# First two units as one 256-column MLP group, a clock model in the ordering loop, and a new table of places

## The chip, the cores and the metric

The kernel runs on one core of a Trainium2 chip. The core has a matrix engine (TensorE, PE in the profile; its weight loads are PEld), a vector engine (VectorE, DVE), a scalar engine (ScalarE, ACT), GpSimd (POOL), and SyncE (SP), whose queue issues nearly all transfers here. Each engine works through its own queue in the order in which the program wrote it. The metric is the device time of one execution in microseconds (us).

## What is computed

Three stages follow each other: a linear recurrence with complex decay (called attention in the code), an MLP with squared ReLU, and a gated MLP behind an RMS norm.

```python
# attention: q, k, v, a_re, a_im are [4, 8, 768, 48]
mag = sqrt(a_re**2 + a_im**2); scale = minimum(mag, 0.999) / (mag + 1e-6)
for t in range(768):
    S_re, S_im = ar*S_re - ai*S_im + k[t] (x) v[t], ar*S_im + ai*S_re
    y[t] = q[t] @ S_re
x = y as [3072, 384]
# MLP 1: w_in [384, 2048], w_out [2048, 384]
x = maximum(x @ w_in, 0)**2 @ w_out
# MLP 2: w_gate, w_val [384, 1536], w_out [1536, 384]
xn = x / sqrt(mean(x*x) + 1e-6) * rms_g
out = (silu(xn @ w_gate) * (xn @ w_val)) @ w_out
```

## The kernel before

**Units.** The sequence is cut into 24 units of 128 positions (4 batches x 6 chunks); unit u belongs to batch u % 4. Each unit goes through these steps. `chain` (L415) builds the decay products on DVE: `norm` with help of ACT, seven steps of `step` (XY, then two A rows, L363 to L370), `tot` (a PE transpose, L380), four levels `plevel` on DVE, `back` (PE, L429), six products, and `inv`. `prod` (L497) makes the tiles KP and QP; `dtr` (L527) transposes them on PE into dk and dq; `score` (L540) multiplies them on PE and masks the result on DVE (st, L542); `yy` or, for units 0 and 1, `yy_direct` (L575) makes the unit's output on PE (yps); `state` (L606) updates the running state. The output becomes the MLP's input xs, split in a high and a low part (L905 and L907 for units 0 and 1, L843 and L845 for the others).

**Chains and groups.** `SETS` says which units share a chain: unit 0 alone, unit 1 alone, then pairs. `GROUPS` says which units share the columns of a matmul of MLP 1: `[0]`, `[1]`, `[2, 3]`, `[4, 5]`, `[6, 7]`, and then four units at a time. So the matmuls of MLP 1 have 128, 128, 256, 256, 256 and from then on 512 columns.

**MLP 1.** For each group there are 16 steps f. `mlp_h` issues nine matmuls (three passes of high and low parts times three row tiles, L943), then ACT computes r (L950), gs (L953) and h (L955), and DVE the low part of gs (L957). `mlp_x` issues nine more (L963) from gs. Nine such matmuls are called a block below. A block of the first group needs the units' xs, and each f its weights: these arrive as 16-bit words and are put together by `convert` (ACT L638, DVE L640 into cr, ACT L870, and the low part on DVE, L882, or for even f on PE, L876 and L877).

**MLP 2.** Six groups of 512 columns, 12 steps f each, of one block g, one block v (L1135) and one block o (L963). us, the input of o, has three buffers.

**What sets the order.** The class `Plan` runs a small list scheduler when the program is written. Each job (a step of one unit, one block, one load) is a generator that yields `Op`s with an engine, a cost and what they need. `Plan.job` gives it a place: a due time from the loops, plus `PRI` of its kind, plus an amount from the table `SHIFT` for the n-th job of that kind. `Plan.run` takes the engine times by its own cost functions, picks among the jobs that could start soonest the one with the lowest place, and writes its instructions. Its order is the order of every engine's queue on the chip. Its costs include a rule on TensorE's clock: after a pause of more than 2.0, the next 3.0 of matmul cost count double (`self.cold`).

Of the kernel before, what the change touches and what calls it, by code (L numbers as in the profile page):

```python
# [1 line left out]

# [20 lines left out]
NU = B * NC  # L23
# [16 lines left out]
    load_a=-32, load_qk=-31, load_v=-28, chain=-32, decay=-32, prod_k=-24, prod_q=-24, join=-24, dtr_k=-24, dtr_q=-24,  # L40
    score=-24, y=-24, fix=-24, split=-24, turned=-24, state=-23.6, mlp_h=-60, mlp_x=-59.9, store_x=-60, load_w=-347,
    convert=-12, load_x=-72, rms=-72, mlp_g=-60, mlp_v=-59.9, mlp_o=-59.8, store=-60, load_w2=-16, convert2=-16,
)
SHIFT = dict(
    chain=((0, 6, 42.5), (6, 11, 30), (11, 12, 29), (12, 13, 28.5),),
    convert=((1, 2, -32.5), (3, 4, -18), (4, 6, -3), (6, 8, -45.5), (8, 16, -3),),
    convert2=((0, 18, -10.5),),
    decay=((0, 8, 60.5), (8, 9, -20.5), (9, 13, 60.5),),
    dtr_k=((2, 7, -38.5), (7, 11, -57.5), (11, 12, -111.5), (12, 21, -92.5), (21, 24, -54),),
    dtr_q=((0, 5, 2.5), (5, 6, -101.5), (6, 13, -34.5), (13, 14, -101.5), (14, 15, -104), (15, 19, -101.5),  # L50
        (19, 21, -104), (21, 23, -114.5), (23, 24, -10.5),),
    fix=((0, 9, 4.5), (9, 11, -1.5), (11, 22, 4.5),),
    join=((36, 38, 7), (48, 102, 48.5), (102, 114, 81),),
    load_a=((7, 11, -62),),
    load_w=((6, 8, -5), (11, 14, -24.5), (14, 15, -13.5), (15, 16, -78.5),),
    mlp_g=((5, 40, -4.5), (40, 47, -7.5),),
    mlp_h=((7, 10, 5), (10, 13, -13.5), (13, 16, 5), (31, 34, 11.5), (76, 78, 28.5),),
    mlp_o=((0, 15, 3), (15, 28, -37.5), (28, 65, 3), (65, 72, 2.5),),
    mlp_x=((55, 58, 46), (126, 128, -1),),
    prod_k=((0, 24, -39),),  # L60
    prod_q=((0, 1, 26), (1, 6, 66.5), (6, 23, 26), (23, 24, 24),),
    rms=((0, 6, 19.5),),
    score=((39, 48, -19),),
    split=((1, 8, 22.5), (8, 9, 49.5),),
    state=((0, 10, 10), (10, 12, 65.5), (12, 13, 40.5), (13, 20, 10),),
    store=((7, 16, -1.5),),
    store_x=((3, 6, 2.5), (16, 18, 50.5),),
    turned=((2, 3, 25.5), (6, 9, 4), (9, 10, -23.5), (10, 11, 17.5), (11, 19, -23.5), (19, 20, 4),),
    y=((13, 24, 22),),
)  # L70
LAND = 2.2
AFTER = {"pe": 0.2, "dve": 0.115, "act": 0.095, "pool": 0.12}
URGENT, NEAR = -250, 0.3
LATE = {"pe": 2.0}
SETS = [[0], [1]] + [[u, u + 1] for u in range(2, NU, 2)]
SET = {u: (s, us.index(u)) for s, us in enumerate(SETS) for u in us}
GROUPS = [[0], [1], [2, 3], [4, 5], [6, 7]] + [list(range(u, u + 4)) for u in range(8, NU, 4)]
OF = {u: (g, us.index(u)) for g, us in enumerate(GROUPS) for u in us}
DIRECT = (0, 1)


def mm(k, n):
    return k * (0.006 + 0.0004375 * n)
# [6 lines left out]
def act(n):  # L90
    return 0.097 + n / 1200


def after(of, to):
    return 0.0 if of == to == "pe" else AFTER.get(of, 0.0)


class Op:


    def __init__(self, eng, cost, need=(), acq=(), rel=(), done=None, mb=0.0, p=0.0, free=False):
        self.eng, self.cost, self.need, self.acq, self.rel = eng, cost, need, acq, rel
        self.done, self.mb, self.p, self.free = done, mb, p, free


class Plan:
# [6 lines left out]
    def __init__(self, counts):  # L113
        self.counts = counts
        self.taken = {r: 0 for r in counts}
        self.back = {r: [] for r in counts}
        self.t = {}
        self.free = {}
        self.bus = 0.0
        self.cold = 0.0  # L120
        self.jobs = []
        self.kinds = {}
        self.log = []

    def job(self, kind, at, gen, need=()):
        n = self.kinds[kind] = self.kinds.get(kind, -1) + 1
        at += PRI[kind] + sum(d for lo, hi, d in SHIFT.get(kind, ()) if lo <= n < hi)
        self.jobs.append([at, len(self.jobs), gen, None, 0.0, need])

    def ready(self, j):  # L130

        t, op = j[4], j[3]
        for n in (*j[5], *op.need):
            end, eng = self.t[n]
            t = max(t, end + after(eng, op.eng))
        for r in op.acq:
            k = self.taken[r] - self.counts[r]
            if k >= 0:
                if k >= len(self.back[r]):
                    return None  # L140
                end, eng = self.back[r][k]
                t = max(t, end + after(eng, op.eng))
        return t

    def run(self):
        live = list(self.jobs)
        while live:
            best = {}
            for j in live:
                if j[3] is None:  # L150
                    if not all(n in self.t for n in j[5]):
                        continue
                    j[3] = next(j[2])
                if not all(n in self.t for n in j[3].need):
                    continue
                r = self.ready(j)
                if r is not None:
                    s = max(r, self.free.get(j[3].eng, 0.0))
                    fresh = r + LATE.get(j[3].eng, 0.0) * (j[3].p == 0.0)
                    best.setdefault(j[3].eng, []).append((s, j[0] + j[3].p, j[1], j, fresh))  # L160
            pick = []
            for c in best.values():
                s0 = min(x[0] for x in c)
                now = [x for x in c if x[0] <= s0 + 0.02]
                now += [x for x in c if s0 + 0.02 < x[0] <= s0 + NEAR and x[1] <= URGENT]
                old = [x for x in now if x[4] <= max(s0, x[0])]
                pick.append(min(old, key=lambda x: x[1:3]) if old else min(now, key=lambda x: (x[4], *x[1:3])))
            s, _, _, j, _ = min(pick, key=lambda x: x[:3])
            op = j[3]
            self.log.append((s, op.eng, op.cost, j[2].__name__, j[0]))  # L170
            cost = op.cost
            if op.eng == "pe":
                if s - self.free.get("pe", 0.0) > 2.0:
                    self.cold = 3.0
                cost += min(cost, self.cold)
                self.cold = max(0.0, self.cold - op.cost)
            end = self.free[op.eng] = s + cost
            for r in op.acq:
                self.taken[r] += 1
            if op.mb:  # L180
                self.bus = max(self.bus, end) + op.mb * 4.0
                end = self.bus + LAND
            for r in op.rel:
                self.back[r].append((end, op.eng))
            if op.done is not None:
                self.t[op.done] = (end, op.eng)
            j[3] = next(j[2], None)
            j[5] = ()
            if j[3] is None:
                live.remove(j)  # L190
            elif j[3].free:
                j[4] = max(j[4], s)
            else:
                j[4] = end + after(op.eng, j[3].eng)
# [616 lines left out]
def kernel_body(ctx: ExitStack, tc, q, k, v, vt, a_re, a_im, w, rms_g, out):  # L811
# [80 lines left out]
    def xs_tile(u):  # L892
        g, i = OF[u]
        if i == 0:
            xs_t[g] = sb.tile([128, 2, KT, len(GROUPS[g]) * CH], F32R, tag="xs", name="xs", bufs=2)
        return xs_t[g]
# [38 lines left out]
    def mlp_h(g, f):  # L935
        n = len(GROUPS[g]) * CH
        yield Op("pe", mm(9, n), acq=["h"], rel=["xs"] if f == F1 - 1 else [], done=("h", g, f), p=MLP_PE)
# [30 lines left out]
    def mlp_x(g, f):  # L968
        n = len(GROUPS[g]) * CH
        yield Op("pe", mm(9, n), acq=[] if f else ["xg"], rel=["gs"], done=("x", g, f), p=MLP_PE)  # L970
        if f == 0:
            x_ps[g] = [psx.tile([128, n], F32, tag=f"x{e}", name=f"x{e}") for e in range(KT)]
        turned_out(x_ps[g], lambda bb: part(f, 1, bb), g_t.pop((g, f)), f == 0, f == F1 - 1)

    def store_x(g, e):
        n = len(GROUPS[g]) * CH
        yield Op("act", act(n), acq=["r"], done=("xc", g, e))
        x = sb.tile([128, n], F32, tag="r", name="x1", bufs=2)
        nc.scalar.copy(out=x, in_=x_ps[g][e])
        yield Op("sp", 0.65, rel=["r"], mb=0.27, done=("xnd", g, e))  # L980
        nc.sync.dma_start(xnd[e * 128:(e + 1) * 128, GROUPS[g][0] * CH:GROUPS[g][0] * CH + n], x)

# [283 lines left out]
```

## Time and profile before

| | us |
|---|---|
| median of 3 runs | 1145.66 |
| lowest, highest | 1144.36, 1145.94 |
| the profiled execution, its own time | 1144.84 |
| its span, first to last instruction | 1142.9 |
| PE busy in the span | 1096.0 (96%) |
| DVE busy | 705.8 (62%) |
| ACT busy | 570.9 (50%) |

The profile is of one execution. A row of a timeline gives the start, the length and the number of equal instructions in a run; since matmuls overlap, the step from one block's start to the next one's start is what a block costs, not its length. The granted clock (PEclk) is a share of TensorE's full 2.4 GHz; 0.50 is its other level, 1.2 GHz. A share of busy time is a mean over a stretch: which engine sets the pace has to be read stretch by stretch.

### The profile page before, as it was taken

The numbers are of one execution on the slowest core, as the hardware profiler recorded it, in microseconds if no ns is written. First come the engines' busy times: TensorE is split into PE (matmuls) and PEld (weight loads), VectorE is DVE, ScalarE is ACT, GpSimd is POOL, SyncE is SP. The second block draws the span as 40 slices with busy tenths as digits, with TensorE's granted clock in tenths as the row PEclk, the third lists the DMA queues.
The fourth block names the chain that finished last, engine by engine and source line by source line (L and its number), as shares of the span: only waits on it lengthen the run. The fifth ranks groups of instructions, "written<-read, shape, count | busy, mean of one in ns | idle before, by whom it ended". The sixth has DMA issues, their size and how long they took to land.

```text
span 1142.9 us, 17676 instructions
## 1 busy us (share of the span) xinstructions
PE 1096.0 (96%) x6850; PEld 931.1 (81%) x6850; DVE 705.8 (62%) x1461; ACT 570.9 (50%) x1142; POOL 4.0 (0%) x14
## 2 busy tenths in 40 slices
PE   2788999999999999999999999999999999999997
PEld 1687899999998888888888888888888888888886
DVE  7969878999999989896522786452252332522221
ACT  4757657768657557554644895242142331421221
POOL 1000000000000000000000000000000000000000
PEclk9778899999999999999999999999999999999999
DMA  9821414423524524301002762001010010000001
GB/s 315 268 72 31 129 45 109 113 76 103 137 63 105 140 57 132 88 26 54 29 2 70 255 207 80 28 1 56 1 56 1 1 56 1 1 28 1 28 1 31
DMA packets 87452, 85.54 MB, mean 75 GB/s; under 512 B 50560, under 2 KB 79168, under 8 KB 87360
## 3 DMA queue, kind: packets, MB, share of 16 engines
q1 hardware_dynamic: 86688, 83.87, 24.4%
q8 instruction: 56, 0.92, 0.3%
q10 hardware_dynamic: 672, 0.46, 0.1%
q14 instruction: 36, 0.29, 0.1%
HBM read 64.61 MB, written 18.61 MB: 73 GB/s over the span
## 4 chain that ended last, share of the span: by engine, by line
PE 89%; DVE 6%; ACT 1%; DMA 1%; SPq 1%; issue 1%; ACTq 0%; DVEq 0%
PE x L963 18%; PE h L943 18%; PE o L963 13%; PE v L1135 13%; PE g L1135 13%; PE sps L540 4%; PE dps L527 3%; PE yps L557 2%; PE ups L606 2%; PE yps L561 1%; PE lo L876 1%; DVE cr L640 1%; DVE KP L497 1%; DVE XY L363 1%; PE tot L380 0%
## 5 line engine op out<-in xcount | busy, mean ns | idle before, releaser
L963 PE MATMUL x<-gs,w 128*128 128x512 f32 (+2 forms) x1296 | 251.1, 342 | 4.9 <-DVE gs L957 3.3
L943 PE MATMUL h<-xs,w 128*128 128x512 f32 (+2 forms) x1296 | 247.1, 337 | 1.9 <-ACT w L879 1.3
L963 PEld LDWEIGHTS x<-gs,w 128*128 128x128 f32 x1296 | 202.5, 198 | 28.6 <-DVE gs L957 3.9
L943 PEld LDWEIGHTS h<-xs,w 128*128 128x128 f32 x1296 | 197.7, 193 | 26.2 <-ACT w L879 1.7
L963 PE MATMUL o<-us,w 128*128 128x512 f32 x648 | 161.2, 395 | 0.0
L1135 PE MATMUL v<-ys,w 128*128 128x512 f32 x648 | 161.0, 393 | 0.0
L1135 PE MATMUL g<-ys,w 128*128 128x512 f32 x648 | 161.0, 393 | 0.0
L963 PEld LDWEIGHTS o<-us,w 128*128 128x128 f32 x648 | 121.8, 188 | 28.7
L1135 PEld LDWEIGHTS v<-ys,w 128*128 128x128 f32 x648 | 121.8, 188 | 27.7
L1135 PEld LDWEIGHTS g<-ys,w 128*128 128x128 f32 x648 | 121.8, 188 | 27.7
L845 DVE TENSOR_TENSOR us<-uu,us 128x512 fp32r<-128x512 f32 x72 | 49.8, 692 | 133.5 <-ACT us L843 133.3
L1155 DVE TENSOR_TENSOR uu<-t,v 128x512 f32<-128x512 f32 x72 | 49.5, 688 | 125.8 <-PE v L1135 123.0
L843 ACT CAST us<-uu 128x512 fp32r<-128x512 f32 x72 | 44.7, 621 | 151.9 <-PE o L963 111.2
L1147 ACT ACTIVATE t<-g 128x512 f32<-128x512 f32 x72 | 43.0, 598 | 140.8 <-PE g L1135 130.7
L953 ACT ACTIVATE gs<-r 128x512 fp32r<-128x512 f32 (+2 forms) x144 | 70.0, 487 | 79.2 <-PE x L963 64.1
L957 DVE TENSOR_TENSOR gs<-h,gs 128x512 fp32r<-128x512 f32 (+2 forms) x144 | 73.2, 510 | 58.4 <-ACT h L955 58.2
L950 ACT ACTIVATE r<-h 128x512 f32<-128x512 f32 (+2 forms) x144 | 65.0, 452 | 73.6 <-PE h L943 69.7
L955 ACT ACTIVATE h<-r 128x512 f32<-128x512 f32 (+2 forms) x144 | 64.6, 450 | 0.0
L540 PE MATMUL sps<-dq,dk 112*128 112x128 f32 x384 | 53.4, 289 | 2.1 <-ACT dk L529 2.1
L540 PEld LDWEIGHTS sps<-dq,dk 112*128 112x128 f32 x384 | 50.7, 203 | 4.5 <-ACT dk L529 2.9
L363 DVE TENSOR_TENSOR XY<-A 128x384 f32<-128x384 f32 (+1 forms) x91 | 47.8, 525 | 1.6
L638 ACT CAST top<-ws 128x384 f16<-128x384 bf16 x68 | 41.4, 626 | 8.4 <-DVE cr L640 7.9
(129 smaller groups left out, 1192.9 us busy)
## 6 DMA issues: line engine op xcount, KB each, us to landing
ws<-in_w SPq DMA_DIRECT2D x34, 767.8 KB, 6.6
kb<-KP SPq DMA_DIRECT2D x20, 448.0 KB, 4.3
kt<-kb SPq DMA_DIRECT2D x20, 448.0 KB, 4.6
raw<-in_a_re SPq DMA_DIRECT2D x24, 192.0 KB, 3.3
kin<-in_k SPq DMA_DIRECT2D x24, 192.0 KB, 3.8
qin<-in_q SPq DMA_DIRECT2D x24, 192.0 KB, 4.0
V<-in_vt SPq DMA_DIRECT2D x24, 192.0 KB, 3.0
xr<-xnd SPq DMA_DIRECT2D x6, 768.0 KB, 4.5
```

The lines of the kernel that those rows point to most:

```text
L363: nc.vector.tensor_tensor(out=T, in0=v.unsqueeze(1).to_broadcast([128, 2, 2, n]), in1=w.unsqueeze(2).to_broadcast([128, 2, 2, n]), op=ALU. ...
L540: nc.tensor.matmul(P[:, i], lhsT=K[:, h, :], rhs=Q[:, h, :], start=True, stop=True)
L843: nc.scalar.copy(out=hi, in_=src)
L845: nc.vector.tensor_tensor(out=lo, in0=src, in1=hi.bitcast(F32), op=ALU.subtract)
L943: nc.tensor.matmul(hp, lhsT=part(f, 0, a)[:, kk * 128:(kk + 1) * 128], rhs=xs[:, bb, kk, :], start=(i == 0), stop=(i == 8),)
L950: nc.scalar.activation(out=r, in_=hp, func=AF.Relu)
L953: nc.scalar.activation(out=gs[:, 0], in_=r, func=AF.Square)
L955: nc.scalar.activation(out=hp, in_=r, func=AF.Square)
L957: nc.vector.tensor_tensor(out=gs[:, 1], in0=hp, in1=gs[:, 0].bitcast(F32), op=ALU.subtract)
L963: nc.tensor.matmul(ps[e], lhsT=w(bb)[:, e * 128:(e + 1) * 128], rhs=src[:, a, :], start=(first and n == 0), stop=(last and n == 2),)
L1135: nc.tensor.matmul(P, lhsT=part(T_GATE + f, half, a)[:, kk * 128:(kk + 1) * 128], rhs=ys[:, bb, kk, :], start=(i == 0), stop=(i == 8),)
L1155: nc.vector.tensor_tensor(out=uu, in0=t_t.pop((g, f)), in1=P, op=ALU.mult)
```

## The change

Three edits are made together. `GROUPS` joins units 0 and 1 to one group `[0, 1]`, while `SETS`, and with it the two separate chains, stays. The rule on the clock in `Plan.run` is replaced by a new method, `clocked`, which keeps its own account of how busy its TensorE was and halves the rate accordingly; it is only used while the program is written and puts no instruction into it. The table `SHIFT` is replaced as a whole, and places are rounded.

```diff
 SHIFT = dict(
-    chain=((0, 6, 42.5), (6, 11, 30), (11, 12, 29), (12, 13, 28.5),),
...
+    chain=((0, 6, -10), (6, 8, -7), (8, 13, -3.5),),
...
 LAND = 2.2
+WINDOW, PHASE, RISE, STAY, SPARSE = 3.4133, 1.5, 0.45, 0.35, 0.45
...
-GROUPS = [[0], [1], [2, 3], [4, 5], [6, 7]] + [list(range(u, u + 4)) for u in range(8, NU, 4)]
+GROUPS = [[0, 1], [2, 3], [4, 5], [6, 7]] + [list(range(u, u + 4)) for u in range(8, NU, 4)]
...
-        self.cold = 0.0
+        self.warm = False
+        self.window = [0, 0.0]
...
+        at = floor(at * 1024 + 0.5) / 1024
         self.jobs.append([at, len(self.jobs), gen, None, 0.0, need])
...
+    def clocked(self, s, cost, dense):
+
+        t, left = s, cost
+        while left > 0:
+            n = floor((t - PHASE) / WINDOW)
+            if n > self.window[0]:
+                busy = self.window[1] / WINDOW if n == self.window[0] + 1 else 0.0
+                self.warm = busy >= (STAY if self.warm else RISE)
+                self.window = [n, 0.0]
+            rate = 1.0 if self.warm else 0.5
+            step = min(left / rate, max(PHASE + (n + 1) * WINDOW - t, 1e-6))
+            self.window[1] += step * (1.0 if dense else SPARSE)
+            left -= step * rate
+            t += step
+        return t - s
...
             if op.eng == "pe":
-                if s - self.free.get("pe", 0.0) > 2.0:
-                    self.cold = 3.0
-                cost += min(cost, self.cold)
-                self.cold = max(0.0, self.cold - op.cost)
+                cost = self.clocked(s, cost, op.p > 0)
             end = self.free[op.eng] = s + cost
```

The whole order of the program moves. Line numbers of the changed kernel are 15 higher than before. Three places are shown; names are those of the tiles above, with buffer numbers, and a matmul of 32-bit data stands once in the order and twice in a trace.

PE before, from the second half of unit 1's transposed KP (dps) to its scores (sps):

```order
L527 MATMUL dps<-ident,KP_94 112x128 x4
L963 MATMUL x_509<-gs,w 128x128 x3
L963 MATMUL x_510<-gs,w 128x128 x3
L963 MATMUL x_511<-gs,w 128x128 x3
L943 MATMUL h<-xs,w 128x128 x18
L963 MATMUL x_509<-gs,w 128x128 x3
L963 MATMUL x_510<-gs,w 128x128 x3
L963 MATMUL x_511<-gs,w 128x128 x3
L540 MATMUL sps<-dq,dk 128x128 x8
```

PE after, from the same transposes to the first block of MLP 1:

```order
L542 MATMUL dps<-ident,KP_94 112x128 x8
L555 MATMUL sps<-dq,dk 128x128 x4
L891 MATMUL lo<-cr,ident 128x384
L892 MATMUL lo<-w,minus 128x384
L555 MATMUL sps<-dq,dk 128x128 x4
L891 MATMUL lo<-cr,ident 128x384
L892 MATMUL lo<-w,minus 128x384
L590 MATMUL yps<-st,Vg 64x128 x12
L395 MATMUL tot<-ident,A_89 48x128 x4
L891 MATMUL lo<-cr,ident 128x384
L892 MATMUL lo<-w,minus 128x384
L958 MATMUL h<-xs,w 128x256 x27
```

Four blocks of unit 0 stood between unit 1's transposes and its scores; now no block of MLP 1 is issued until both units' outputs (yps) are.

DVE before, behind unit 1's KP:

```order
L497 TENSOR_TENSOR KP_94<-A_90,kin 128x16x48
L957 TENSOR_TENSOR gs<-h,gs 128x128 x2
L368 TENSOR_TENSOR A_89<-XY 128x96
L370 TENSOR_TENSOR A_89<-XY 128x96
L640 SCALAR_TENSOR_TENSOR cr<-ws,top_67 128x384
L363 TENSOR_TENSOR XY<-A_89 128x384
```

DVE after, behind the same instruction:

```order
L512 TENSOR_TENSOR KP_94<-A_90,kin 128x16x48
L385 TENSOR_TENSOR A_89<-XY 128x96
L897 TENSOR_TENSOR w<-cr,w 128x384
L378 TENSOR_TENSOR XY<-A_89 128x384
L897 TENSOR_TENSOR w<-cr,w 128x384
L383 TENSOR_TENSOR A_89<-XY 128x96
```

The 128-column gs rows, which wait for a block and for ACT, are gone from between the rows of the chain of units 2 and 3; the same chain and weight rows follow without them.

PE before, at the first block of the group `[2, 3]`:

```order
L527 MATMUL dps<-ident,QP 112x128 x4
L963 MATMUL x_1509<-gs,w 128x128 x3
L963 MATMUL x_1510<-gs,w 128x128 x3
L963 MATMUL x_1511<-gs,w 128x128 x3
L943 MATMUL h<-xs,w 128x128 x9
L963 MATMUL x_1509<-gs,w 128x128 x3
L963 MATMUL x_1510<-gs,w 128x128 x3
L963 MATMUL x_1511<-gs,w 128x128 x3
L943 MATMUL h<-xs,w 128x256 x9
```

PE after, at the same place (the first nine of the 27 are the last h block of `[0, 1]`):

```order
L891 MATMUL lo<-cr,ident 128x384
L892 MATMUL lo<-w,minus 128x384
L958 MATMUL h<-xs,w 128x256 x9
L978 MATMUL x_786<-gs,w 128x256 x3
L978 MATMUL x_787<-gs,w 128x256 x3
L978 MATMUL x_788<-gs,w 128x256 x3
L542 MATMUL dps<-ident,QP 112x128 x8
L958 MATMUL h<-xs,w 128x256 x27
```

The last weights of MLP 1 (lo) are now put together just ahead of this place, and the 128-column blocks that filled PE's queue there are gone.

## Rows read from the trace of the kernel before

**Rows 1.** Stretches: us, each engine's busy time (instructions), granted clock, DMA share, GB/s.

```profile
core 0: us, PE busy (x) PEld busy (x) DVE busy (x) ACT busy (x) POOL busy (x), PEclk, DMA share, GB/s
0.00:45.00 45.00, 18.25 (x83) 12.73 (x83) 35.52 (x118) 24.03 (x52) 4.03 (x14) 0.92 0.91 303
45.00:64.05 19.05, 15.36 (x73) 12.35 (x73) 18.75 (x48) 15.96 (x41) 0.00 (x0) 0.72 0.57 192
64.05:89.10 25.05, 24.90 (x182) 23.96 (x183) 16.25 (x45) 12.44 (x30) 0.00 (x0) 0.67 0.30 82
89.10:171.72 82.62, 75.34 (x654) 69.54 (x653) 70.82 (x171) 51.37 (x143) 0.00 (x0) 0.92 0.23 63
171.72:336.74 165.02, 163.83 (x1687) 157.67 (x1688) 157.48 (x355) 113.55 (x280) 0.00 (x0) 1.00 0.38 102
336.74:432.00 95.26, 94.40 (x669) 78.03 (x667) 86.96 (x190) 59.90 (x118) 0.00 (x0) 1.00 0.35 94
432.00:600.00 168.00, 168.00 (x1167) 140.54 (x1165) 114.68 (x220) 94.52 (x173) 0.00 (x0) 1.00 0.20 56
600.00:1100.00 500.00, 500.00 (x2195) 407.31 (x2194) 197.07 (x309) 191.81 (x298) 0.00 (x0) 1.00 0.15 50
```

**Rows 2.** PE's timeline at full clock, 128 and 256 columns: start us, length, instructions.

```profile
165.28 1.17 PE L963 MATMUL x<-gs,w 128*128 128x128 f32 x9
166.29 1.17 PE L943 MATMUL h<-xs,w 128*128 128x128 f32 x9
...
304.46 1.24 PE L963 MATMUL x<-gs,w 128*128 128x256 f32 x9
305.54 1.24 PE L943 MATMUL h<-xs,w 128*128 128x256 f32 x9
```

**Rows 3.** PE's timeline, the first h of groups [0], [2, 3] and [8 to 11].

```profile
45.05 1.22 PE L943 MATMUL h<-xs,w 128*128 128x128 f32 x9 [0.41 <-DVE xs L907]
...
171.72 0.46 PE L943 MATMUL h<-xs,w 128*128 128x256 f32 x2
...
337.15 0.50 PE L943 MATMUL h<-xs,w 128*128 128x512 f32 x1
```

**Rows 4.** DVE's timeline: KP and xs of units 0 and 1, xs of unit 11.

```profile
30.82 0.96 DVE L497 TENSOR_TENSOR KP<-A,kin 128x768 f32<-128x768 f32 x1
...
44.44 0.55 DVE L907 SCALAR_TENSOR_TENSOR xs<-yps,xs 128x384 fp32r<-128x384 f32 x1
...
63.09 0.96 DVE L497 TENSOR_TENSOR KP<-A,kin 128x768 f32<-128x768 f32 x1
...
88.54 0.55 DVE L907 SCALAR_TENSOR_TENSOR xs<-yps,xs 128x384 fp32r<-128x384 f32 x1
...
336.19 0.56 DVE L845 TENSOR_TENSOR xs<-xt,xs 128x384 fp32r<-128x384 f32 x1
```

**Rows 5.** What DVE waited for, 45 to 336.74 us: total, times, longest.

```profile
DVE gs L957 <- ACT h L955: 9.2, 13, 1.3
DVE st L542 <- PE sps L540: 4.7, 4, 3.0
...
DVE cr L640 <- ACT top L638: 2.1, 2, 1.9
```

**Rows 6.** DVE's groups by shape, 0 to 337 us: busy, mean ns | idle before.

```profile
L957 DVE TENSOR_TENSOR gs<-h,gs 128x256 fp32r<-128x256 f32 x48 | 20.1, 420 | 0.4 <-ACT h L955 0.3
...
L957 DVE TENSOR_TENSOR gs<-h,gs 128x128 fp32r<-128x128 f32 x32 | 9.1, 289 | 9.1 <-ACT h L955 9.0
```

**Rows 7.** PE's timeline of 128-column blocks, and a PE stretch (busy, clock, DMA).

```profile
71.47 4.04 PE L943 MATMUL h<-xs,w 128*128 128x128 f32 x18
...
72.00:76.00 4.00, 4.00 (x21) 0.50 0.02 4
```

**Rows 8.** PE's timeline in MLP 2: a g block, and the last four o blocks.

```profile
814.03 2.21 PE L1135 MATMUL g<-ys,w 128*128 128x512 f32 x9
...
1127.41 8.47 PE L963 MATMUL o<-us,w 128*128 128x512 f32 x36
```

More of the change, by code (lines that the diff above doesn't have):

```diff
@@ L1 @@
 from contextlib import ExitStack
+from math import floor
 import concourse.bass as bass
@@ L44 @@
 SHIFT = dict(
-    chain=((0, 6, 42.5), (6, 11, 30), (11, 12, 29), (12, 13, 28.5),),
[L46 to L69, printed above, removed]
+    chain=((0, 6, -10), (6, 8, -7), (8, 13, -3.5),),
+    convert2=((16, 18, -4),),
+    decay=((0, 2, -2.5), (2, 3, -25.5), (3, 12, -5), (12, 13, -2.5),),
@@ new lines @@
+    dtr_k=((0, 11, -3.5), (11, 22, -20.5), (22, 24, -3.5),),
+    dtr_q=((7, 8, -5), (8, 9, -7.5), (9, 16, -2.5), (16, 17, -22), (17, 18, -2.5), (18, 21, -15.5),
+        (21, 24, -13),),
+    fix=((1, 12, 0.5), (12, 13, 30.5), (13, 14, 6.5), (14, 15, 0.5),),
+    join=((0, 113, 3),),
+    load_v=((0, 26, 31),),
+    load_w=((4, 6, 26), (6, 8, 5), (8, 16, 26),),
+    load_w2=((14, 16, 2.5), (16, 18, -51.5),),
+    load_x=((2, 3, 2.5),),
+    mlp_h=((22, 83, 1), (84, 98, 0.5),),
+    mlp_o=((0, 72, 20),),
@@ L70 @@
+    mlp_v=((0, 7, 4.5), (7, 13, -46.5), (13, 72, 4.5),),
+    prod_q=((9, 10, 5.5),),
+    rms=((0, 2, 55), (2, 3, -7), (3, 5, -26.5),),
+    score=((16, 26, -9.5),),
+    split=((0, 22, -44.5),),
+    state=((1, 4, -15), (6, 9, 16), (9, 10, 25), (10, 11, 16), (11, 13, 45.5), (13, 14, 16), (14, 15, 49),),
+    store_x=((4, 5, -47.5), (10, 23, 28),),
+    turned=((9, 16, -4),),
+    y=((14, 17, -1.5), (17, 18, -3), (18, 22, -1.5), (22, 23, -7.5), (23, 24, -1.5),),
 )
 LAND = 2.2
+WINDOW, PHASE, RISE, STAY, SPARSE = 3.4133, 1.5, 0.45, 0.35, 0.45
```

## The prediction

> **What bounds the kernel now.** I read the stretches first [rows 1]. From 171.72 us to 1100 us PE is busy for 926 of 928 us at full clock, so in that part time goes only if PE work goes, or if the same work starts earlier. In front of it PE is the lesser engine: up to 171.72 us it is busy for 133.9 us at a mean clock between 0.67 and 0.92, and waits for DVE's chains. DVE is busy for 298.8 us up to 336.74 us (the sum of the first five stretches) and idle for 9.5 us before 45 us and for 28.4 us after; between 171.72 and 336.74 us it is busy for 157.5 of 165.0 us. So DVE is the second engine with almost nothing to spare until the group of units 8 to 11 begins, and has plenty later (86.96 of 95.26 us, then 114.7 of 168.0).
>
> The second view is PE's timeline at the groups' first blocks [rows 3] beside DVE's at the tiles that free them [rows 4]. Unit 0's block starts at 45.05 us, when its xs is done (44.44 us plus 0.55). Unit 11's xs ends at 336.75 us, and the first 512-column block starts at 337.15 us, 0.4 us later. From there to the end the two kernels have the same PE work. So the forecast comes down to one number: when does the first 512-column block start?
>
> **What the change does to PE.** It removes work. Nine matmuls of 128 columns step 1.01 us (165.28 to 166.29), nine of 256 columns 1.08 us (304.46 to 305.54) [rows 2]. Before, units 0 and 1 take 2 x 32 blocks, 64.3 us at full clock; after, 32 blocks, 34.6 us. The gain is 29.7 us of PE time, and that is an upper end: a block that ran where PE had nothing else to do gains nothing.
>
> The Trainium skill, page "TensorE: Matmul & The Clock Gate", section "Back-to-back issue gap", speaks against this edit: it gives 134 cycles for a matmul of 128 columns and 262 for one of 256 at full clock, so that two narrow ones cost about as much as a wide one. By it (an estimate from that page) 288 pairs would save 6 cycles each, under 1 us in all. The trace disagrees: narrow and wide blocks differ by 0.07 us [rows 2]. I take the rows, and nothing below rests on the page.
>
> What it takes away is cover. Between 45 and 89 us PE worked on unit 0's blocks; now it has no block until unit 1's xs is there. That idle time costs nothing by itself, since PE isn't the bound there, provided that unit 1 comes earlier. It does. Before, KP of unit 1 ends at 64.05 us and its xs at 89.1 us [rows 4]: 25.05 us in which DVE is busy for only 16.25 us [rows 1]. PE is busy all through, at clock 0.67, because its queue has four blocks between unit 1's transposes and its scores, one run of 18 matmuls alone taking 4.04 us [rows 7]; DVE's st waits behind that [rows 5]. After, scores follow the transposes with only weight work (lo) between. For unit 0, which had no blocks in its way, the same path took 13.2 us (KP's end at 31.78 us to xs's end at 44.99 us) [rows 4]. DVE has some 14 us of own rows in that place in the new order, and unit 1's KP comes about 2.5 us earlier (by the order, two gs rows, three cr rows and two w rows fewer in front of it). So xs of unit 1: 61.5 + 14 + 1.5 for waits = 77 us, where it was 89.1.
>
> **What it does to DVE.** I counted in the two orders what DVE has before unit 11's xs. 32 gs rows of 128 columns go and 16 of 256 come: 9.1 us out, 16 x 0.42 = 6.7 us in [rows 6]. Against that, three products KP or QP (0.96 us each [rows 4]) and three rows of the same size ahead of them come earlier, and some ten rows of a later chain, each under 0.6 us, go later; these net to between 1 and 3 us more. The sum is 0, give or take 1 us: DVE must still do 298.8 us of work before unit 11's xs. So DVE can gain only from its idle time.
>
> How much of the 37.9 us of idle time goes? The first 9.5 us stay: the first rows of both orders are alike. Of the 28.4 us behind 45 us, 9.0 are gs rows of 128 columns waiting for ACT's h; the 48 gs rows of 256 columns waited 0.3 us in all [rows 6]. I take 1 us for the 16 new ones. st waiting for sps cost 4.7 us, one wait 3.0 [rows 5], of which I take 2.7 away with the blocks in front of unit 1's scores; and the 2.1 us of cr waiting for ACT's top fell mostly in the same 25 us, where ACT itself waited for blocks. That leaves 28.4 - 9.0 + 1.0 - 2.7 - 2.1 = 15.6 us. Hence unit 11's xs at 298.8 + 0 + 9.5 + 15.6 = 323.9 us and the first 512-column block 0.4 us later, at 324.3 us: 12.8 us earlier than 337.15.
>
> The bounds. At best DVE is idle for half the share that it has between 171.72 and 336.74 us (7.5 of 165 us, 4.6%); over 285 us that is 6.5 us, and the block starts 22 us earlier. At worst it idles as before, 28.4 us, and nothing is gained. I stay near the middle because the rows name each wait that goes.
>
> **Can PE follow?** Between 171.72 and 337.15 us PE did 96 blocks of 256 columns, 103.7 us, so the attention of the eight units in that time took the other 61.7 us, 7.7 us a unit. After its first block at about 77.5 us PE has, by the order, 32 blocks (34.6 us), the attention of two units (15.4 us) and a few lo rows (I take 3 us) before the first block of units 2 and 3: 53 us, to 130.5 us. But the last weights of MLP 1 are made late in the new order, right ahead of that block. DVE has about 70 us of rows between unit 1's xs and the last of them (some 150 instructions of the order, each at the length that its shape has in the trace); with 5 us of waits that is 152 us. From that block to the 512-column block PE took 165.4 us before (171.72 to 337.15) [rows 3], with the same work after: 152 + 165.4 = 317.4 us. That is 7 us ahead of DVE, so DVE decides, narrowly.
>
> **The clock.** PE with gaps may be given half the clock. The rows say that being busy is not enough: from 72 to 76 us PE was busy for 4.00 of 4.00 us with 128-column blocks at clock 0.50 [rows 7]. The Trainium skill's page on TensorE's clock gate, section "Why this matters for your kernels", advises to keep TensorE busy without a break to have full clock; this row goes against it. I cost the clock at 4 us of PE time when the blocks begin, which is within the waiting for weights up to 152 us; uncovered it would be 4 us.
>
> **The rest.** `clocked` and the rounding issue no instruction: 0. In MLP 2 the new table puts three o blocks in a row instead of one between v and g. Nine matmuls of o in a row step 2.1 us, as do alternating blocks (8.47 us for four; 2.21 us with its overlap for a g block) [rows 8]; us has three buffers, so three o blocks need no more than there is. I take 0, with 2 us either way. Loads stay in the same order on SP's queue up to unit 1's tiles.
>
> **The sum.** The profiled execution took 1144.84 us; 12.8 us less is 1132.0 us. It lies 0.8 us below the median of the runs, 1145.66, so the forecast for the median is 1132.8 us.
>
> **The rivals.**
> Rival 1, PE sets the pace: DVE's idle time shrinks to 6 to 9 us behind 45 us because PE, with less in its queue, answers at once. Then PE's 317.4 us decides, 19.7 us less: 1126 us, in a range from 1116 (weights early too) to 1127 us. For it: DVE's small idle share later. Against it: before unit 1's xs and up to 152 us DVE and ACT still wait for each other in the chain.
> Rival 2, the wait moves: DVE is as idle as before because the new order puts other waits in its queue, at ups, back or tot, in place of gs. Then unit 11's xs stays at about 336 us and PE simply idles where its blocks were: 1144 to 1147 us, no change. For it: gs, st and cr explain 16.0 of the 28.4 us [rows 5]; the other 12.4 us come from many places, and new ones can be opened.
> Rival 3, slower: the 16 gs rows of the joint group stand in DVE's queue among the chains of units 2 to 5, behind PE blocks that themselves come in bursts. If each waits as long as the longest wait for ACT's h, 1.3 us [rows 5], that is 20.8 us, and idle time becomes 28.4 - 9.0 + 20.8 = 40.2 us: the 512-column block comes 12 us later, 1158 us. With nothing else gained it decides from 0.6 us for each gs; the mean of the 32 narrow ones was 0.28 us [rows 6]. Against it: 0.3 us for 48 wide ones.
> The Trainium skill's rule on narrow matmuls gives a rival of its own: no PE time saved, and so no earlier start than rival 2's; the rows leave it no chance.
>
> **How the numbers follow.** Forecast (start 6 to 18 us earlier, 1127 to 1140 us): 0.60. Rival 1: 0.15. Between 1140 and 1143 us, faster still: 0.04. Rival 2: 0.11. Rival 3: 0.10. The range from 1123 to 1145 us takes in the forecast, the nearer half of rival 1 and the nearer part of rival 2. 0.2% is 2.3 us, about what a measurement of this kernel can tell from no change. Faster: 0.60 + 0.15 + 0.04 = 0.79; same: 0.11; slower: 0.10.
>
> **What would show it.** Right: xs of unit 1 near 77 us, with no block of MLP 1 before; the first 256-column block of units 2 and 3 near 152 us; unit 11's xs and the first 512-column block within a microsecond of each other near 324 us; DVE's idle time between 45 us and there about 16 us; waits of gs for ACT's h near 1 us; from there to the end the same time as before. Wrong: unit 1's xs later than 85 us; PE's clock at 0.50 behind 90 us for long; the 512-column block starting well after unit 11's xs (PE decides, rival 1 or the clock); gs waits above 8 us (rival 3); or a gap in MLP 2 ahead of the three o blocks.

## The result, and the profile after

| | before | after |
|---|---|---|
| median of 4 runs, us | 1145.72 | 1125.91 |
| lowest, highest | 1144.36, 1145.94 | 1124.99, 1126.61 |
| the profiled execution, its span | 1144.84, 1142.9 | 1126.14, 1124.4 |

The changed kernel takes 0.9829 of the time of before, 95% interval 0.9812 to 0.9846: 19.8 us less, where 12.9 us less was forecast. The time lies in the range, and the sign was right; one term of the sum was too large. It lies 1.1 us below the 1127 to 1140 us to which the forecast itself gave 0.60, and is the time that rival 1 gave (1126 us), so the question for the runs is which engine now decides.

Line numbers of after are 15 higher. Its stretches, cut at the same events as those of [rows 1] (us, busy time and instructions of PE, PEld, DVE, ACT and POOL, granted clock, DMA share, GB/s); 76.28 us is the end of unit 1's xs, 147.40 us lies in the last h block of the group [0, 1], right ahead of the first block of units 2 and 3, and 319.30 us is the end of unit 11's xs. The last row is a cut of its own, for the chain below:

```profile
0.00:45.00 45.00, 19.16 (x82) 13.28 (x82) 36.56 (x124) 24.36 (x52) 3.57 (x14) 0.81 0.93 301
45.00:76.28 31.28, 17.20 (x116) 12.12 (x114) 29.76 (x73) 19.72 (x39) 0.47 (x1) 0.73 0.59 187
76.28:147.40 71.12, 59.79 (x506) 54.10 (x506) 68.81 (x156) 53.52 (x122) 0.00 (x0) 0.91 0.26 70
147.40:319.30 171.90, 166.31 (x1691) 158.88 (x1689) 164.09 (x364) 118.35 (x286) 0.00 (x0) 1.00 0.37 100
...
177.65:319.75 142.10, 140.08 (x1440) 134.66 (x1441) 135.59 (x298) 97.60 (x235) 0.00 (x0) 1.00 0.37 99
```

DVE is busy for 29.76 of the 31.28 us before unit 1's xs, where it had 16.25 of 25.05 us in the stretch ahead of that xs before. PE is the idle one there, for 14.1 us; with DVE full, that sets nothing. From 147.40 us both engines are nearly full: PE 166.31 and DVE 164.09 of 171.90 us.

The places that answer to [rows 3] and [rows 4], from the timelines of PE and DVE of after (start, length, instructions, idle time ahead with its releaser). The nine matmuls from 146.22 us are the last h block of the group [0, 1]; they end at 148.19 us, and since matmuls overlap, the block of units 2 and 3 starts near 148.0 us:

```profile
75.72 0.56 DVE L922 SCALAR_TENSOR_TENSOR xs<-yps,xs 128x384 fp32r<-128x384 f32 x1 [1.22 <-ACT xs L920]
...
75.74 1.46 PE L958 MATMUL h<-xs,w 128*128 128x256 f32 x8
...
146.22 1.97 PE L958 MATMUL h<-xs,w 128*128 128x256 f32 x9
...
318.75 0.55 DVE L860 TENSOR_TENSOR xs<-xt,xs 128x384 fp32r<-128x384 f32 x1
...
319.35 0.65 PE L542 MATMUL dps<-ident,KP 128*112 128x128 f32 x4 [0.68 <-ACT dk L544]
319.75 1.62 PE L958 MATMUL h<-xs,w 128*128 128x512 f32 x6
```

The first 512-column block starts at 319.75 us instead of 337.15 us, 17.4 us earlier. It starts 0.45 us behind unit 11's xs, and the row above it says that PE is no longer waiting for xs alone: the block stands behind a transpose that waited 0.68 us for ACT's copy of the one before. Behind the block's start lie 804.65 us of span, 805.75 us before. So 17.4 of the 18.5 us of span are gained ahead of this point, and 1.1 us behind it.

The chain of work that ended last, followed back from this block, holds these rows of DVE and ACT from 177 us on (start, length); all the rest of it is PE's own instructions:

```profile
177.26 0.35 DVE gs L972
...
264.57 0.59 ACT dq L544
...
317.39 0.59 ACT dq L544
318.71 0.59 ACT dk L544
```

So PE last takes up the pace from DVE at 177.65 us, and is then busy for 140.08 of the 142.10 us up to the block. By this view PE sets the last 142 us; DVE is nearly full beside it (135.59 us). Which of the two has time to spare, the first two runs below tell.

What DVE waited for between 45 and 319.30 us (total, times, longest), against [rows 5]:

```profile
DVE m L331 <- ACT A L329: 1.4, 2, 1.1
DVE st L557 <- PE sps L555: 1.3, 2, 0.8
...
DVE gs L972 <- ACT h L970: 0.9, 3, 0.4
```

Its gs rows by shape, up to 320 us (busy, mean ns | idle before), against [rows 6]; all of them are 256 columns wide now:

```profile
L972 DVE TENSOR_TENSOR gs<-h,gs 128x256 fp32r<-128x256 f32 x64 | 26.7, 419 | 1.7 <-ACT h L970 0.9
```

gs waits 0.9 us in all where it waited 9.2 us; cr no longer waits for top at all; st waits 1.3 us instead of 4.7 us.

### The profile page after: what moved, and what is told of

Its sections match the earlier page's. It is cut to its first block, busy times and chain, and to the rows that moved or that the text cites. A ratio compares the mean times of both kernels' runs of the same rounds, so it can differ in the third digit from the quotient of the medians.

```text
span 1124.4 us, 16870 instructions
## 1 busy us (share of the span) xinstructions
PE 1059.1 (94%) x6562; PEld 892.0 (79%) x6562; DVE 706.1 (63%) x1445; ACT 563.1 (50%) x1091; POOL 4.0 (0%) x14
## 4 chain that ended last, share of the span: by engine, by line
PE 88%; DVE 7%; ACT 1%; DMA 1%; issue 1%; SPq 0%; DVEq 0%; ACTq 0%
PE x L978 17%; PE h L958 17%; PE o L978 13%; PE g L1150 13%; PE v L1150 13%; PE sps L555 4%; PE dps L542 3%; PE yps L572 2%; PE ups L621 2%; PE yps L576 2%; DVE x L458 1%; PE tot L395 1%; DVE A L458 1%; DVE cr L655 0%; DVE XY L378 0%
## 5 line engine op out<-in xcount | busy, mean ns | idle before, releaser
L958 PE MATMUL h<-xs,w 128*128 128x256 f32 (+1 forms) x1152 | 228.1, 344 | 11.1 <-DVE gs L972 10.7
L978 PE MATMUL x<-gs,w 128*128 128x256 f32 (+1 forms) x1152 | 228.5, 344 | 4.1 <-DVE gs L972 3.2
L958 PEld LDWEIGHTS h<-xs,w 128*128 128x128 f32 x1152 | 180.1, 191 | 36.0 <-DVE gs L972 12.0
L978 PEld LDWEIGHTS x<-gs,w 128*128 128x128 f32 x1152 | 180.6, 191 | 28.8 <-DVE gs L972 4.0
L978 PE MATMUL o<-us,w 128*128 128x512 f32 x648 | 154.4, 395 | 0.0
L965 ACT ACTIVATE r<-h 128x256 f32<-128x256 f32 (+1 forms) x128 | 62.5, 489 | 100.9 <-PE h L958 97.6
L972 DVE TENSOR_TENSOR gs<-h,gs 128x256 fp32r<-128x256 f32 (+1 forms) x128 | 70.7, 553 | 48.5 <-ACT h L970 47.6
L968 ACT ACTIVATE gs<-r 128x256 fp32r<-128x256 f32 (+1 forms) x128 | 67.0, 524 | 30.9 <-PE x L978 25.0
L970 ACT ACTIVATE h<-r 128x256 f32<-128x256 f32 (+1 forms) x128 | 62.1, 485 | 0.0
```

Of the source, the lines that this page charges most:

```text
L958: nc.tensor.matmul(hp, lhsT=part(f, 0, a)[:, kk * 128:(kk + 1) * 128], rhs=xs[:, bb, kk, :], start=(i == 0), stop=(i == 8),)
L965: nc.scalar.activation(out=r, in_=hp, func=AF.Relu)
L968: nc.scalar.activation(out=gs[:, 0], in_=r, func=AF.Square)
L970: nc.scalar.activation(out=hp, in_=r, func=AF.Square)
L972: nc.vector.tensor_tensor(out=gs[:, 1], in0=hp, in1=gs[:, 0].bitcast(F32), op=ALU.subtract)
L978: nc.tensor.matmul(ps[e], lhsT=w(bb)[:, e * 128:(e + 1) * 128], rhs=src[:, a, :], start=(first and n == 0), stop=(last and n == 2),)
```

## The experiments

The theory: DVE's busy time and idle time up to unit 11's xs set the start of the 512-column block, and everything behind it is fixed. The rival: PE, with its 166 us of work from 147.4 us on, sets it. Beside that stood the question which of the three edits brings the gain. The runs were taken in three groups, and before, run again beside each, took 1145.35, 1145.10 and 1145.81 us (medians). The changed kernel was not run again, so differences from its 1125.91 us are good to about 1 us.

### Ten DVE instructions more, and ten fewer, in the changed kernel

In the same order of instructions, ten products of 768 columns in the chains of units 2 to 11 are added, or left out.

```diff
-            nc.vector.tensor_tensor(out=o, in0=i0, in1=i1, op=ALU.mult)
+            for _ in range(3 if n == 0 and 2 <= p <= 6 else 1):
+                nc.vector.tensor_tensor(out=o, in0=i0, in1=i1, op=ALU.mult)
```

> The changed kernel with 10 more DVE instructions of 768 columns (one product of the chains of units 2 to 11 written three times), 8.7 us of DVE work before unit 11's xs, the order otherwise the same. Theory D (DVE sets the start of the 512-column block): 7 to 9 us slower than the changed kernel, 1133 to 1135 us, unit 11's xs near 328 us and the block within 1 us of it. Rival P (PE sets it, as the time of 1125.9 us would say by rival 1 of the prediction): at most 3 us slower, 1126 to 1129 us.

```diff
-            nc.vector.tensor_tensor(out=o, in0=i0, in1=i1, op=ALU.mult)
+            if n < 2 or not 2 <= p <= 6:
+                nc.vector.tensor_tensor(out=o, in0=i0, in1=i1, op=ALU.mult)
```

> The changed kernel without 10 DVE instructions of 768 columns (two products of the chains of units 2 to 11 are left out, so that the output isn't the reference's), 8.7 us of DVE work less before unit 11's xs. Theory D: faster by 5 to 9 us, 1117 to 1121 us; less than 8.7 us because PE was idle for only 5.6 us between 147.4 and 319.3 us. Rival P: within 2 us of 1125.9 us.

Measured: 1135.88 us with ten more (10.0 us over the changed kernel), 1122.84 us with ten fewer (3.1 us under it). First the stretches of the kernel with ten more, then that with ten fewer, cut at the 76 us of unit 1 and at unit 11's xs or the 512-column block:

```profile
45.00:76.00 31.00, 18.53 (x115) 13.59 (x115) 29.41 (x71) 19.24 (x39) 0.00 (x0) 0.67 0.63 200
76.00:329.71 253.71, 228.33 (x2194) 214.08 (x2194) 242.55 (x529) 172.21 (x406) 0.00 (x0) 0.96 0.32 88
```

```profile
76.00:317.50 241.50, 228.07 (x2199) 215.21 (x2199) 225.52 (x510) 172.52 (x406) 0.00 (x0) 0.96 0.34 92
...
147.40:317.42 170.02, 166.03 (x1690) 159.05 (x1690) 159.15 (x356) 118.00 (x285) 0.00 (x0) 1.00 0.38 102
```

Added DVE work comes out in full: 9.6 us more busy time up to unit 11's xs (308.8 against 299.2 us; 36.86 us of the 308.8 lie before 45 us), and a time 10.0 us longer, 1 us above theory D's range. So DVE has nothing to spare. Removed work comes out for a third only, between the two expectations: 3.1 us of time, 2.3 us at the block. The block of units 2 and 3 starts near 147.3 us instead of 148.0 us, and from there to the 512-column block the way shrinks from 171.7 us to 170.1 us; from 147.40 us on PE is busy for 166.03 of 170.02 us, and DVE is idle in place of busy. Its waits, in the kernel with ten fewer, up to 317.5 us:

```profile
DVE gs L973 <- ACT h L971: 3.0, 7, 0.9
DVE St L630 <- PE ups L622: 2.1, 3, 1.1
DVE Y L634 <- PE ups L622: 1.4, 1, 1.4
```

These are waits for what PE makes, the first by way of ACT. So the two engines are level within some 3 us: with more DVE work DVE decides, with less of it PE does, and neither theory holds alone. In the changed kernel as it is, the chain above is PE's from 177.65 us on, with a DVE beside it that can't take a delay.

### The joint group alone

Before, with only `GROUPS` changed; entries of the old table that count blocks are renumbered for 16 fewer.

```diff
-GROUPS = [[0], [1], [2, 3], [4, 5], [6, 7]] + [list(range(u, u + 4)) for u in range(8, NU, 4)]
+GROUPS = [[0, 1], [2, 3], [4, 5], [6, 7]] + [list(range(u, u + 4)) for u in range(8, NU, 4)]
...
-    mlp_x=((55, 58, 46), (126, 128, -1),),
+    mlp_x=((39, 42, 46), (110, 112, -1),),
...
```

> The kernel before with only the joint group [0, 1]; the old table (its entries for MLP 1 renumbered for the missing group) and the old clock rule stay. Theory A (the joint group itself gives the gain, since it takes 29.7 us of PE work and the gs waits of 9.0 us off DVE): at least half of the gain, 1126 to 1136 us, with unit 1's xs before 80 us. Rival B (the places give it; in the old ones the new group's blocks fall where DVE or PE must wait): 1142 us or more, with DVE idle for over 25 us between 45 us and unit 11's xs.

Measured: 1139.70 us, a ratio of 0.995 (0.9932 to 0.9968) to before: 5.6 us of the 19.8, between the two expectations. PE's timeline at the first 512-column block of this kernel:

```profile
324.28 1.65 PE L943 MATMUL h<-xs,w 128*128 128x512 f32 x3 [4.34 <-ACT xs L843]
326.23 2.65 PE L943 MATMUL h<-xs,w 128*128 128x512 f32 x6 [0.29 <-DVE xs L845]
```

Two stretches behind it, of the same kernel:

```profile
324.28:345.00 20.72, 19.66 (x95) 15.43 (x96) 20.43 (x50) 13.16 (x28) 0.00 (x0) 0.90 0.45 118
345.00:500.00 155.00, 151.36 (x1136) 125.36 (x1135) 139.82 (x282) 93.33 (x174) 0.00 (x0) 1.00 0.31 85
```

The group alone brings the block's start 12.9 us forward, about what was forecast for the whole change, with unit 1's xs at 75.86 us. But its first three matmuls need only the high part of xs; the low part of unit 11's ends at 326.18 us, 10.6 us earlier than before, and the other six wait for it. And half of the 12.9 us is not there at the end: this block is followed by 812.1 us of span, 6.4 us more than in before. PE idles 3.6 us in the 155 us from 345 us on, and the clock falls to 0.90 for a while. That places of the old table behind this point were made for blocks that come later is the likely reason; no run tests it.

### The group undone under the new table and rule

```diff
-GROUPS = [[0, 1], [2, 3], [4, 5], [6, 7]] + [list(range(u, u + 4)) for u in range(8, NU, 4)]
+GROUPS = [[0], [1], [2, 3], [4, 5], [6, 7]] + [list(range(u, u + 4)) for u in range(8, NU, 4)]
...
-    mlp_h=((22, 83, 1), (84, 98, 0.5),),
+    mlp_h=((38, 99, 1), (100, 114, 0.5),),
...
```

> The changed kernel with units 0 and 1 as two groups again; the new table (its entries for MLP 1 renumbered) and the new clock rule stay. Theory A (the joint group gives the gain): it is lost, 1140 us or more, gs rows of 128 columns wait for ACT's h for over 6 us. Rival B (the places give it): at most 1135 us.

Measured: 1199.92 us, a ratio of 1.049 (1.0465 to 1.0515) to before; the 512-column block starts at 392.65 us. A stretch of this kernel:

```profile
180.00:200.00 20.00, 20.00 (x97) 20.00 (x96) 7.87 (x13) 8.81 (x24) 0.00 (x0) 0.50 0.00 0
```

Its two shapes of gs, up to 393 us:

```profile
L972 DVE TENSOR_TENSOR gs<-h,gs 128x256 fp32r<-128x256 f32 x48 | 20.0, 417 | 6.9 <-ACT h L970 6.8
L972 DVE TENSOR_TENSOR gs<-h,gs 128x128 fp32r<-128x128 f32 x32 | 9.1, 286 | 25.8 <-ACT h L970 25.7
```

This is worse than either kernel, so the edits don't add up: the table is only good with the groups that it was searched for. Theory A's signs came. A part of the loss has a visible cause: PE works through 128-column blocks without a gap, 20.00 of 20.00 us, at half clock, and DVE waits 25.7 us for the 128-column h and 6.8 us for the 256-column one. DVE is idle for 73.6 us between 45 and 393 us, so these waits are not all of it.

### The same ten DVE instructions in the kernel before

```diff
-            nc.vector.tensor_tensor(out=o, in0=i0, in1=i1, op=ALU.mult)
+            for _ in range(3 if n == 0 and 2 <= p <= 6 else 1):
+                nc.vector.tensor_tensor(out=o, in0=i0, in1=i1, op=ALU.mult)
```

> The kernel before with the same 10 more DVE instructions as in the run with more DVE work (8.7 us before unit 11's xs). If PE alone set the pace before, 0 to 3 us slower, 1146 to 1149 us, DVE's idle time falling by the 8.7 us. If DVE set it before too, 6 to 9 us slower, 1152 to 1155 us.

Measured: 1168.95 us, 23.6 us over the runs of before on the same chip (1145.35 us), for some 9 us of work. Neither expectation held. PE's timeline of this kernel:

```profile
163.13 1.22 PE L944 MATMUL h<-xs,w 128*128 128x128 f32 x9 [1.25 <-DVE gs L958]
...
169.62 2.12 PE L944 MATMUL h<-xs,w 128*128 128x128 f32 x9
171.54 2.12 PE L964 MATMUL x<-gs,w 128*128 128x128 f32 x9
...
195.75 2.36 PE L944 MATMUL h<-xs,w 128*128 128x256 f32 x18
```

A stretch of it, and then the same stretch of before:

```profile
170.00:180.00 10.00, 10.00 (x49) 10.00 (x49) 4.67 (x10) 3.56 (x11) 0.00 (x0) 0.50 0.00 0
```

```profile
170.00:180.00 10.00, 9.33 (x81) 8.56 (x81) 7.69 (x16) 6.22 (x18) 0.00 (x0) 1.00 0.27 74
```

What DVE waited for, from 45 to 363 us, in the kernel with ten more:

```profile
DVE gs L958 <- ACT h L956: 20.7, 15, 3.2
```

In this run the last 128-column blocks stand one behind the other, where before had begun its 256-column blocks at 171.72 us [rows 3]. They step 1.92 us instead of the 1.01 us of [rows 2], with the engine busy for 10.00 of 10.00 us; they end soon after the first 256-column block, at 191.49 us. DVE's gs rows wait 20.7 us in all, where they waited 9.2 us [rows 5]. Ahead of the fall PE had waited 1.25 us for a gs; why the clock fell here and not in before is not settled by these rows. That it fell, and that blocks then took nearly twice as long, is. In the changed kernel the same ten instructions cost 10.0 us. So in before a delay of DVE turned into half-clock blocks, which delayed DVE again, and in the changed kernel it didn't. That this is the joint group's doing is likely, since it leaves no 128-column blocks, but the two kernels differ in all three edits.

### The rule on the clock

The changed kernel with the old rule put back; group and table stay.

```diff
-                cost = self.clocked(s, cost, op.p > 0)
+                if s - self.free.get("pe", 0.0) > 2.0:
+                    self.cold = 3.0
+                cost += min(cost, self.cold)
+                self.cold = max(0.0, self.cold - op.cost)
...
```

> The changed kernel with the old clock rule in the ordering loop; joint group and new table stay. If the clock account matters only as the rule that the places were searched with, any other rule shifts the order and costs: 1130 to 1150 us. If the joint group is what counts and the order's details don't: 1124 to 1130 us.

Measured: 1134.30 us, 8.4 us over the changed kernel, in the range of the first theory. That could be the worth of a better rule, or only that the table was searched with the new one. Two more runs bear on this: the new rule with another offset. No trace here speaks for one offset or another.

```diff
-WINDOW, PHASE, RISE, STAY, SPARSE = 3.4133, 1.5, 0.45, 0.35, 0.45
+WINDOW, PHASE, RISE, STAY, SPARSE = 3.4133, 0.0, 0.45, 0.35, 0.45
```

> The changed kernel with one constant of the planner's clock rule changed, PHASE 0 in place of 1.5: the rule itself, the groups and the table stay. Nothing in it follows the chip better or worse than before, since the program cannot know the offset on the chip; only the order comes out another. Theory M, the table fits only the rule it was searched with: DVE's idle time between 45 us and unit 11's xs grows from 11.6 us to some 15 to 20 us and the time is 1129 to 1136 us, as with the old rule (1134.3). Theory F, the new rule describes TensorE better than the old one, and any offset does: idle time 10 to 13 us, 1124.5 to 1128 us.

```diff
-WINDOW, PHASE, RISE, STAY, SPARSE = 3.4133, 1.5, 0.45, 0.35, 0.45
+WINDOW, PHASE, RISE, STAY, SPARSE = 3.4133, 2.25, 0.45, 0.35, 0.45
```

> As the run with PHASE 0, with PHASE 2.25. Theory M: 1129 to 1136 us, with DVE's idle time behind 45 us at 15 to 20 us. Theory F: 1124.5 to 1128 us, idle time 10 to 13 us. If one offset gives the one and another the other, the table is matched to an order, and the 8.4 us that the old rule costs are luck of the order rather than the rule's worth.

Measured: 1138.65 us and 1132.44 us, so 12.7 and 6.5 us over the changed kernel, the old rule's 8.4 us lying between. The second lies in theory M's range, the first above it. Stretches up to unit 11's xs: the old rule's, then offset 0, then offset 2.25:

```profile
73.97:326.84 252.87, 231.95 (x2234) 218.67 (x2234) 236.83 (x530) 174.80 (x415) 0.00 (x0) 0.97 0.33 90
```

```profile
74.41:332.48 258.07, 233.32 (x2228) 217.32 (x2228) 238.61 (x529) 172.65 (x411) 0.00 (x0) 0.97 0.33 90
```

```profile
76.14:326.46 250.32, 233.00 (x2220) 220.04 (x2221) 233.08 (x520) 169.72 (x406) 0.00 (x0) 0.96 0.33 89
```

PE's clock is the same in all of them (0.96 or 0.97; 0.97 in the changed kernel's stretch from 76.28 to 319.30 us). What differs is DVE: its idle time from 45 us on is 16.3, 19.9 and 18.1 us, against 11.6 us, and it has 301.3, 304.3 and 299.8 us of work placed ahead of unit 11's xs, against 299.2 us. So these runs give no sign that the new rule is the better one. They show that the table fits one order, and that any other rule makes another order of it. What the rule would bring with a table of its own search is open. The joint group with the new rule under the old table has no run: there the loop that sets the order comes to a point at which no job can start.

### DVE work given to other engines

If DVE alone decides, 8.7 us of it (16 low parts of weights, 552 ns each) might go elsewhere. To PE, which makes the low parts of even f already:

```diff
-ON_PE = range(0, F1, 2)
+ON_PE = range(0, F1)
```

> The changed kernel with the low parts of all 16 weights of MLP 1 made on PE, not of every second one: 16 DVE rows of 384 columns (7.5 us) go from DVE before 152 us, and PE gets 16 lo groups of 0.8 us (13 us) where it is idle for 11.3 us (76 to 147 us) and more before. Theory D (DVE decides): 2 to 7 us faster, 1119 to 1124 us, unless the order that follows is worse. Rival P (PE decides): slower by 3 to 13 us.

Measured: 1132.02 us, 6.1 us slower. DVE's work up to 324.0 us falls to 293.3 us, but its idle time from 45 us on is 21.5 us, with pX waiting 5.5 us for ACT's TP and gs 4.9 us for h. The time lies in the range that the expectation gave to rival P, PE decides. Whether PE's added work did this, or the order that came out, the run can't tell. To GpSimd:

```diff
-                yield Op("dve", dve(DM), rel=[cr] if z else [], free=z == 1, done=("w", n, z))
+                on = ("pool", nc.gpsimd) if early else ("dve", nc.vector)
+                yield Op(on[0], dve(DM) * (2 if early else 1), rel=[cr] if z else [], free=z == 1, done=("w", n, z))
...
```

> The changed kernel with the low parts of the odd weights of MLP 1 made on GpSimd in place of DVE: 16 rows of 384 columns (7.5 us) leave DVE, and nothing is added to PE. Theory D: 3 to 7 us faster, 1119 to 1123 us, unless GpSimd is so slow that blocks wait for the weights or DVE's own rows get longer beside it. Rival P: no change, 1124 to 1128 us.

Measured: 1128.01 us, 2.1 us slower. Two GpSimd rows of this kernel, two DVE rows of the same 128x96 form that lie beside them, and the PE row that waited for the first GpSimd row:

```profile
144.22 4.66 POOL L898 TENSOR_TENSOR w<-cr,w 128x384 fp32r<-128x384 f32 x1 [11.79 <-ACT w L885]
...
148.84 1.02 POOL L898 TENSOR_TENSOR w<-cr,w 128x384 fp32r<-128x384 f32 x1
...
145.10 0.25 DVE L385 TENSOR_TENSOR A<-XY 128x96 f32<-128x96 f32 x1
...
148.92 1.05 DVE L385 TENSOR_TENSOR A<-XY 128x96 f32<-128x96 f32 x1
...
148.93 1.01 PE L959 MATMUL h<-xs,w 128*128 128x256 f32 x3 [3.38 <-POOL w L898]
```

DVE loses 16 rows and is busy for no less: 300.3 us up to unit 11's xs. Its 39 rows of this line between 79.6 and 321.7 us take 304 ns in the mean; in the changed kernel it is 251 ns. And one h block waits 3.38 us for a weight from GpSimd. So DVE was not relieved, and the run says nothing for or against either theory. In both runs the order around the moved rows was not searched for them, so they say only that neither move pays by itself.

## Why the prediction was right, and where it was off

**The frame held.** One number, the start of the first 512-column block, makes the time: in before, after and all runs here except the joint group alone, 803 to 808 us of span follow it. In after unit 11's xs and the block lie 0.45 us apart.

**Unit 1.** Forecast 77 us, measured 76.28 us. KP ends at 60.58 us (61.5), and from there to xs it takes 15.7 us (14 + 1.5). No block of MLP 1 comes before, as the order said.

**DVE's work.** Forecast 298.8 + 0 us, measured 36.56 + 29.76 + 232.89 = 299.2 us. Counting the rows that an order moves past a point, with the lengths of [rows 4] and [rows 6], was good to half a microsecond.

**DVE's idle time: the term that was mis-sized.** Forecast 9.5 us before 45 us and 15.6 us after; measured 8.4 and 11.6 us. That is 5.1 us less, and with 0.4 us more work it makes the 4.6 us by which unit 11's xs comes earlier than forecast (319.30 against 323.9 us). The waits that were named went about as priced: gs 0.9 us (1.0, with 0.2 left of the old ones), st 1.3 us (2.0), cr none (none). The term that was wrong is the rest: of 28.4 us the working explained 16.0 and carried the other 12.4 us over unchanged. Measured, 11.6 - 0.9 - 1.3 = 9.4 us are left, 3.0 us less; the named waits make the other 1.0 us. The three other orders of the same groups stand at 16.3, 18.1 and 19.9 us, above the 15.6 us. That reads as if the forecast had priced the new groups in an order of the usual quality, and the searched order did better by 4 us; what ended the single waits of the rest, no run here separates. An order printed without times doesn't show it.

**Rival 1** gave the measured time: DVE's idle time at 6 to 9 us, and PE's 317.4 us deciding. Its engine is half right. "DVE decides, narrowly" holds against added work, but the chain is PE's from 177.65 us on, and with less DVE work PE decides. DVE idled for 11.6 us, more than the rival said. PE's 317.4 us (319.75 us measured) came near by two errors that nearly cancel: the block of units 2 and 3 came near 148.0 us and not at 152 us (DVE idled 2.3 us in that stretch, with 5 us priced), and the way from there to the 512-column block took 171.7 us, not 165.4 us. That the rival's time fits to 0.1 us is luck. In the working PE was 7 us ahead of DVE; in the runs the two are level within 3 us.

**Rivals 2 and 3** didn't come: waits at ups, back and tot stayed under 1 us each, and gs waits were 0.9 us, not 20.8. What separates the joint group alone from the whole change is 4.5 us at the block's start (324.28 against 319.75 us) and 7.5 us of span behind it (812.1 against 804.65 us), so rival 2's worry about what a new order brings was not idle, though most of it came behind the place that the forecast looked at.

**PE's price.** No run here isolates PE's share. That the 32 blocks of 256 columns and all else fit in ahead of 147.4 us, with PE idle for 11.3 of the last 71 us, agrees with a price of some 1.1 us for a block. The prediction held the table of cycles in the Trainium skill's section "Back-to-back issue gap" (page "TensorE: Matmul & The Clock Gate") against this edit. That section gives it for an isolated matmul and says that at few columns it under-counts, since it leaves no time for loading weights, so it speaks less against the edit than the prediction said. The rows agree with that: 1.01 us for nine narrow matmuls is 112 ns each, twice what 134 cycles take [rows 2].

**The clock.** The 4 us had no row behind them. Between 76.28 and 147.40 us PE has a mean clock of 0.91 and 11.3 us of idle time, which fits that they were hidden; no run tests it.

**MLP 2.** Forecast 0 with 2 us either way; measured 1.1 us less for all that follows the first 512-column block. In before PE was busy for 500.00 of 500 us from 600 us on [rows 1]; after has one wait of 1.5 us there, ahead of MLP 2. The o blocks in a row step 2.1 us up to the end (54 matmuls, six blocks), as priced from [rows 8]. PE's timeline of after:

```profile
604.18 2.34 PE L958 MATMUL h<-xs,w 128*128 128x512 f32 x9 [1.52 <-DVE gs L972]
...
1104.89 12.66 PE L978 MATMUL o<-us,w 128*128 128x512 f32 x54
```

## What to carry to other kernels

Find the event behind which nothing changes, and forecast its time as busy plus idle time of the engine that leads to it. Here busy time could be counted from the new order to half a microsecond; idle time could not, so price the waits you can name and leave several microseconds either way for the rest. Busy plus idle time adds up on every engine, so this sum doesn't say which one decides: add work to one engine and take work from it, and read the chain that ended last. Here that showed two engines that are level. Where a search made the order, its parts can't be priced one by one: here the group alone gave 5.6 us, the new order without the group took 55 us more than before, and a changed constant in the planner 6 to 13 us, so a part of a searched change should be taken over only together with a new search.

## What the runs showed of the hardware

- 128-column blocks back to back stood at half clock with TensorE busy for 20.00 of 20.00 us (the group undone) or 10.00 of 10.00 us (ten rows more in before). They step 1.92 us then, not the 1.01 us that the same blocks take at full clock in before [rows 2]. The Trainium skill's page "TensorE: Matmul & The Clock Gate", section "Why this matters for your kernels", advises keeping the engine busy; in these rows it was, and the clock stood at 0.50 all the same.
- Beside a GpSimd instruction, DVE rows of 0.25 us took up to 1.05 us, and the GpSimd rows themselves took 1.43 us in the mean (median 1.09 us, the longest 4.66 us) for what DVE does in 0.55 us. In this run the work moved to GpSimd was paid for on DVE.
- An order can amplify a delay: some 9 us of DVE work cost 23.6 us in the kernel before, and 10.0 us in the changed one.
